# RetNet attention into a mixture of experts on one core: loads of v on ScalarE's queue, and the second routing round in another order

## The chip, the cores and the metric

The kernel runs on one core of a Trainium2 chip. The core has TensorE (PE in the profile, its weight loads PEld), VectorE (DVE), ScalarE (ACT), GpSimd (POOL) and SyncE (SP), and 16 DMA engines that all of its queues share. The metric is the time on the device in microseconds; lower is better. Each engine takes its instructions in the order in which they are written, so an instruction that waits holds back all that stand behind it on its engine; this goes for DMA issues too.

## The reference, cut to what matters

q, k and v are 4 batches x 8 heads x 768 tokens x 64. The attention's output, 3072 tokens of 512 numbers, goes through a gate, which sends each token to one of eight experts.

```python
def _attn_ref(q, k, v):
    gamma = 1.0 - 2.0 ** (-5.0 - np.arange(H))
    for t in range(S):
        state = gamma * state + np.einsum('bhd,bhe->bhde', k[:, :, t], v[:, :, t])
        y[:, :, t] = scale * np.einsum('bhd,bhde->bhe', q[:, :, t], state)

def _moe_ref(x, w_gate, w1, w2):
    logits = x @ w_gate
    expert_idx = np.argmax(logits, axis=1)
    probs = np.exp(logits - logits.max(-1, keepdims=True)); probs /= probs.sum(-1, keepdims=True) + 1e-09
    gate_w = probs[np.arange(N), expert_idx]
    for e in range(E):                                   # x, y sorted by expert
        y[lo:hi] = np.maximum(x[lo:hi] @ w1[e], 0.0) @ w2[e]
    return gate_w[:, None] * y                           # back in the tokens' order
```

## The kernel before, in words

The attention is done in chunks of 128 tokens. A **step** `s` of the loop (12 of them) takes one chunk of two batches, b = 0 and 1. In a step TensorE does, in this order: `scores` (`sc`, both batches), `with_state` (`y` from the state of the chunks before), on odd steps `logits` of two earlier steps (`parts`), `turn_k` for the next step (`trk`), on odd steps the turn of the logits back (`lg`) and `turn_q` for the next two steps (`trq`), `next_state` (`new`), and `within` (`y` from the masked scores and v, in two halves of 16 products). The other engines stand between these:

- **ScalarE** copies from PSUM what TensorE needs next: `qT` and `kT` for `sc`, `lgT` for `lg`, and `xT`, the step's output, from `y`.
- **VectorE** masks the scores (`am`, two for each batch), adds the state, turns `xT` into rows (`to_rows`, `xg`, three buffers) and does the routing.
- **GpSimd** multiplies q and v by powers of the decay (`qs`, `vs`; the last step's v in place), and later gathers rows.
- **SyncE** issues nearly all transfers, one behind the other: two q of 512 KB on odd steps for three steps ahead, two k of 256 KB for three steps ahead, two v of 256 KB for two steps ahead, then `store` of an earlier step's `xg` to `x_d` (four transfers). ScalarE's queue has one transfer before, `dec`, at the start.

A transfer issued from SyncE or ScalarE is given one of eight semaphores (DMAHW0 to DMAHW7), and it is issued only when the transfer that had the semaphore before has landed. Which one that was is decided when the program is built.

Routing goes in three rounds. A round (`place(i)`) is a Python generator that is cut into pieces by `yield`; `WHEN` says at which of a step's places (letters) the next piece is taken. The second round works on the tokens of steps 5 to 8 and runs in steps 9 and 10. Its pieces: the one-hot choice `ohs` and the gate; `rk`, 9 products that count tokens (L703 to L708) and VectorE's ranks behind them; `val` (L737); `here` (L730, 8 instructions); `found`, 8 products (L746); and last `inv` and the row numbers `src_e`, with which GpSimd gathers the early rows and then scales the last step's v.

```python
WHEN = {5: "abc", 6: "b", 7: "ab", 8: "pp", 9: "aw", 10: "nmbb"}
within(s, y, am, early_rows if s + 1 == STEPS else lambda: step(s, "w"))   # "w": between the halves
```

Of the kernel before, what the change touches and what calls it, by code (L numbers as in the profile page):

```python
# [21 lines left out]
P = 128  # L22
# [24 lines left out]
def middle(ap, n):  # L47

    dims = [list(d) for d in ap.ap]
    return bass.AP(tensor=ap.tensor, offset=ap.offset, ap=[dims[0], [0, n]] + dims[1:])  # L50
# [3 lines left out]
def kernel(  # L54
# [11 lines left out]
    nc = tc.nc  # L66
# [13 lines left out]
    STEPS = NT // 2  # L80
    NEXT = (0, 5, 9, STEPS)
    NR = len(NEXT) - 1
# [73 lines left out]
    def more_of_weights1(w1t, e, parts, now):  # L156
        for part in (ts(i, F // parts) for i in now):
            nc.sync.dma_start(w1t[:, :, :, part], w1v[:, ds(e, 1), :, part])
# [323 lines left out]
    with ExitStack() as actx:  # L482
# [19 lines left out]
        def load(nm, s, b, parts=1):  # L502
            m, b1, e = where[s]
            src = {"q": q, "k": k, "v": v}[nm]
            if nm == "q":
                to = att.tile([P, H, 2 * D], F32, tag=nm, name=nm, bufs=4)
                for part in (ts(i, H // parts) for i in range(parts)):
                    nc.sync.dma_start(to[:, part, :], src[2 * b1 + b, part, ts(m, 2 * P), :].rearrange(
                        "h (t e) d -> t h (e d)", e=2))
            else:  # L510
                to = att.tile([P, H, D], F32, tag=nm, name=nm, bufs=8)
                nc.sync.dma_start(to, src[2 * b1 + b, :, ts(2 * m + e, P), :].rearrange("h t d -> t h d"))
            raw[nm, s, b] = to

        def scale_q(s, b, by=nc.gpsimd, parts=1):
# [22 lines left out]
        def pairs_of(tag, bufs, name):  # L538
            return ps(tag, bufs, name).rearrange("p (a t) -> p a t", a=HP)
# [18 lines left out]
        def q_of(s, b):  # L558
            return qT2[b][:, :, ts(where[s][2], P // 2), :].rearrange("p a t e -> p a (t e)")

        def scores(s, b):
            kT, qT = front.pop((s, b)), q_of(s, b)
            sc = [pairs_of("sc", 4, "sc") for _ in range(2)]
            am = [att.tile([P, HP, P], F32, tag=f"am{j}", name=f"am{j}") for j in range(2)]
            for a in range(HP):
                for j in range(2):
                    r = ts(j, D)
                    nc.tensor.matmul(sc[j][:, a, :], lhsT=kT[r, a, :], rhs=qT[r, a, :], start=True, stop=True)  # L568

            def mask():  # L570
                for j in range(2):
                    nc.vector.tensor_tensor(out=am[j], in0=sc[j], in1=middle(causal[:, :], HP), op=ALU.mult)  # L572

            return am, mask
# [55 lines left out]
        def to_rows(s):  # L630
            xg = x["g", s] = keep.tile([P, 2, Q, DT * L], F32, tag="xg", name="xg", bufs=3)
            for b in range(2):
                nc.vector.transpose(xg[:, b, :, :].rearrange("p r (a l) -> p a r l", l=L),
                                    x[s][:, :, b, :].rearrange("p a (r l) -> p a r l", l=L))
# [157 lines left out]
        am = [scores(0, 0)]  # L792
# [15 lines left out]
                copy(out=xTa[:, :, ts(t, P)], in_=tr)  # L808

        rest = iter(())  # L810
        WHEN = {5: "abc", 6: "b", 7: "ab", 8: "pp", 9: "aw", 10: "nmbb"}

        def step(s, at):
            for _ in range(WHEN.get(s, "").count(at)):
                next(rest, None)

        for s in range(STEPS):
            if s + 3 < STEPS:
                if s % 2:
                    load_all("q", s + 3)  # L820
                load_all("k", s + 3)
                load_all("v", s + 2)
            if s % 2 == 0 and s + 2 < STEPS:
                for b in range(2):
                    scale_q(s + 2, b)
            if s + 2 < STEPS and s != NEXT[NR - 1]:
                scale_both(s + 1)
            if s == NEXT[NR - 1] + 1:
                scale_both(s)
            if s in (1, 2):  # L830
                nc.gpsimd.memset(xs2[s % 2], 0.0)
            if s:
                am = [scores(s, b) for b in range(2)]
                step(s, "n")
                for _, mask in am:
                    mask()
                step(s, "m")
            if s + 1 == STEPS:
                pad_ranks(acc[:, NR - 1, 0:2])
            y = outputs()  # L840
            steps = [i for i in (s - 2, s - 1) if i >= 0] if s % 2 else []
            if s + 1 == STEPS:
                logit = logits(steps)
            if where[s][0] or where[s][2]:
                with_state(s, y)

            def ahead():
                for b in range(2):
                    turn_k(s + 1, b)

            def ahead_q():
                if s % 2:
                    for b in range(2):
                        turn_q(s + 1, b)

            if s:
                if s + 1 < STEPS:
                    if steps:
                        logit = logits(steps)
                    ahead()  # L860
                if s + 1 == STEPS:
                    for t in range(HALF):
                        nc.scalar.copy(out=xe[:, t, :].rearrange("p (a q l) -> p q a l", q=Q, l=L),
                                       in_=xs2[0][:, t, :].rearrange("p (q a l) -> p q a l", q=Q, l=L))
                reduce = logits_of(*logit) if steps else lambda: None
                step(s, "p")
                if s + 1 < STEPS:
                    ahead_q()
                to_rows(s - 1)
                reduce()  # L870
                if 2 <= s <= NEXT[NR - 1]:
                    store(s - 2)
                if s == NEXT[NR - 1]:
                    store(s - 1)
                if s + 1 == STEPS:
                    store(s - 1)
                if s + 1 == STEPS:
                    store(NEXT[NR - 1])
                    wa.append(weights2(first, 0, 2, [0]))
                if s == NEXT[NR - 1]:  # L880
                    load_all("v", STEPS - 1)
                    wa = [weights1(first, 0, 4, [0])]
                if s in NEXT:
                    rest = chain(rest, place(NEXT.index(s) - 1))
                step(s, "a")
            next_state(s)
            step(s, "b")
            if s == NEXT[NR - 1] + 1:
                more_of_weights1(wa[0], 0, 4, [1])
                more_of_weights1(wa[0], 0, 2, [1])  # L890
            within(s, y, am, early_rows if s + 1 == STEPS else lambda: step(s, "w"))
            if s == 0:
                ahead()
            step(s, "c")
# [320 lines left out]
```

## Time and profile before

| | us |
|---|---|
| median of 3 runs (lowest, highest) | 444.47 (444.21, 445.1) |
| the profiled execution's own time | 444.41 |
| its span in the trace | 442.3 |
| TensorE busy in the span | 423.5 |
| mean granted clock of TensorE, share of full speed | 0.996 |

The profiled execution's time and the median lie 0.06 us apart; 2.1 us of the time lie outside the span. TensorE is idle for 442.3 - 423.5 = 18.8 us of the span. In the rows below a line reads: start, duration, engine, line, operation, output<-inputs, and in brackets the engine's idle time just before and the work whose end ended it. "SPq" and "ACTq" are transfers' issues on those engines.

### The profile page before, as it was taken

To read this page: it belongs to the slowest core of one execution; us is meant where nothing else is said; L and a number is where in the kernel's file an instruction comes from. 1 tells how busy PE (TensorE), PEld (TensorE's weight loads), DVE (VectorE), ACT (ScalarE), POOL (GpSimd) and SP (SyncE) were. 2 spreads that over 40 slices of the span, in tenths; PEclk is the share of its full clock that TensorE was granted. 3 is DMA by queue.
4 is the path that set the end of the run, shared out by engine and by line. 5 is a ranking of instruction groups with operands and counts; after the bars stand their busy time and mean duration, and the time that the engine had idled before them with its cause. 6 is when DMAs were issued, how large, how long until landed. Compare 5 with 4: busy or idle time off the path is not lost.

```text
span 442.3 us, 9832 instructions
## 1 busy us (share of the span) xinstructions
PE 423.5 (96%) x3643; PEld 371.3 (84%) x3643; DVE 241.8 (55%) x541; ACT 124.4 (28%) x285; POOL 272.5 (62%) x226
## 2 busy tenths in 40 slices
PE   6899999999999999999999999999899999999992
PEld 3798888877688779689989999997899999699681
DVE  3454686979689937624553563365256346433320
ACT  2355355453421211312310221133122123102310
POOL 4458444544137379397548956899795798679011
PEclk9999999999999999999999999999999999999998
DMA  9999998998982799368134951596594268120001
GB/s 195 221 243 210 240 256 184 251 227 206 275 244 77 246 396 350 82 237 283 35 74 116 371 160 45 156 367 146 158 368 113 52 193 307 33 92 0 5 30 53
DMA packets 113324, 80.68 MB, mean 182 GB/s; under 512 B 56874, under 2 KB 97834, under 8 KB 113200
## 3 DMA queue, kind: packets, MB, share of 16 engines
q1 hardware_dynamic: 104336, 65.31, 52.9%
q0 software_dynamic: 5520, 12.60, 8.8%
q10 hardware_dynamic: 3344, 1.36, 1.3%
q8 instruction: 49, 0.80, 0.8%
q14 instruction: 75, 0.61, 0.4%
HBM read 60.88 MB, written 15.99 MB: 174 GB/s over the span
## 4 chain that ended last, share of the span: by engine, by line
PE 80%; DMA 7%; DVE 3%; SPq 3%; issue 2%; ACT 1%; POOL 1%; ACTq 1%; POOLq 0%; DVEq 0%
PE p L343 25%; PE p L389 17%; PE p L277 8%; PE p L264 6%; PE p L979 6%; PE sc L568 4%; PE y L622 3%; SPq L640 2%; PE yp L389 2%; PE new L604 2%; PE trk L536 2%; PE trq L536 2%; DMA x_d<-xg 2%; DMA w2t<-in_moe_w_dram 2%; DMA q<-in_q_dram 1%
## 5 line engine op out<-in xcount | busy, mean ns | idle before, releaser
L177 POOL DMA_INDIRECT xs<-x_d,src x30 | 31.8, 1060 | 19.0 <-issue 7.2
L347 DVE TENSOR_TENSOR hT<-p,q 128x196 f32<-128x196 f32 (+5 forms) x72 | 25.9, 360 | 31.4 <-PE p L343 31.3
L572 DVE TENSOR_TENSOR am<-sc,causal 128x512 f32<-128x512 f32 x48 | 29.9, 682 | 18.1 <-PE sc L568 18.0
L436 POOL DMA_INDIRECT out_dram<-o,dst x20 | 19.9, 996 | 31.1 <-ACT o L285 12.0
L526 POOL TENSOR_TENSOR vs<-v,dec 128x512 f32<-128x512 f32 x21 | 22.8, 1102 | 24.4 <-DMA v<-in_v_dram 21.5
L389 PE MATMUL p<-ws,hs 128*128 128x256 f32 x168 | 37.5, 380 | 0.4 <-issue 0.4
L277 PE MATMUL p<-w2t,hT 128*24 128x128 f32 (+5 forms) x288 | 37.6, 357 | 0.0
L389 PEld LDWEIGHTS p<-ws,hs 128*128 128x128 f32 x168 | 31.9, 190 | 4.9 <-issue 0.7
L343 PE MATMUL p<-t,w1t 128*128 128x196 f32 (+5 forms) x192 | 35.8, 330 | 0.0
L343 PE MATMUL p<-t,s 128*128 128x196 f32 (+5 forms) x192 | 35.8, 330 | 0.0
L395 DVE SCALAR_TENSOR_TENSOR q<-p,gate,q 128x256 f32<-128x256 f32 x28 | 12.9, 480 | 38.2 <-ACT q L404 24.4
L520 POOL TENSOR_TENSOR qs<-q,dec 128x512 f32<-128x512 f32 x22 | 22.3, 1044 | 18.0 <-DMA q<-in_q_dram 10.9
L305 POOL TENSOR_TENSOR ws<-w2t,ws 128x1024 f32<-128x1024 f32 x14 | 33.0, 2360 | 0.5
L305 POOL TENSOR_TENSOR ws<-w2t 128x1024 f32<-128x1024 f32 x14 | 33.1, 2364 | 0.1
L343 PEld LDWEIGHTS p<-t,w1t 128*128 128x128 f32 x192 | 32.4, 190 | 0.0
L343 PEld LDWEIGHTS p<-t,s 128*128 128x128 f32 x192 | 32.4, 190 | 0.0
L277 PEld LDWEIGHTS p<-w2t,hT 128*24 128x24 f32 (+5 forms) x288 | 18.5, 123 | 16.1 <-issue 14.8
L347 DVE TENSOR_TENSOR q<-p,q 128x196 f32<-128x196 f32 (+5 forms) x48 | 17.1, 358 | 25.6 <-PE p L343 18.4
L395 DVE SCALAR_TENSOR_TENSOR o<-p,gate,q 128x256 f32<-128x256 f32 x21 | 10.2, 484 | 35.4 <-PE p L389 35.4
L568 PE MATMUL sc<-qT,kT 64*128 64x128 f32 x384 | 24.9, 279 | 2.3 <-ACT kT L555 2.3
L389 PE MATMUL p<-w2t,hT 128*128 128x256 f32 x112 | 26.9, 382 | 0.1
L568 PEld LDWEIGHTS sc<-qT,kT 64*128 64x128 f32 x384 | 22.5, 188 | 4.6 <-ACT kT L555 3.0
(221 smaller groups left out, 888.3 us busy)
## 6 DMA issues: line engine op xcount, KB each, us to landing
w1t<-in_moe_w_dram SPq DMA_DIRECT2D x7, 2048.0 KB, 8.7
w2t<-in_moe_w_dram SPq DMA_DIRECT2D x7, 2048.0 KB
k<-in_k_dram SPq DMA_DIRECT2D x24, 256.0 KB, 6.0
v<-in_v_dram SPq DMA_DIRECT2D x24, 256.0 KB, 4.3
x_d<-xg SPq DMA_DIRECT2D x48, 128.0 KB, 3.3
q<-in_q_dram SPq DMA_DIRECT2D x11, 512.0 KB, 6.5
xs<-xs SPq DMA_DIRECT2D x80, 64.0 KB, 2.2
w2t<-in_moe_w_dram SPq DMA_DIRECT2D x2, 1024.0 KB
```

The lines of the kernel that those rows point to most:

```text
L177: nc.gpsimd.indirect_dma_start(out=xs[:, t, :], out_offset=None, in_=x_d[0:rows, :], in_offset=bass.IndirectOffsetOnAxis(ap=idx[:, t : t + ...
L264: nc.tensor.matmul(hp, lhsT=w1t[:, 0, dt, ts(f, P)], rhs=xT[:, dt, n0:n], start=(dt == 0), stop=(dt == DT - 1))
L277: nc.tensor.matmul(y[j * z : j * z + m, 0:c], lhsT=hT[:, f, t * P + r0 : t * P + r0 + m], rhs=w2t[:, 0, f, ts(j, c)], start=(i == 0), stop ...
L305: by.tensor_tensor(out=ws[i], in0=sums[i][0], in1=sums[i][1], op=ALU.subtract)
L343: nc.tensor.matmul(rows(y), lhsT=a(d, f), rhs=b(d), start=start and d == 0, stop=d == 1, skip_group_check=True)
L347: nc.vector.tensor_tensor(out=to, in0=rows(y), in1=rows(plus), op=ALU.add)
L389: nc.tensor.matmul(y, lhsT=a[:, f, :], rhs=b[:, f, :], start=start and f == 0, stop=f == FH - 1, skip_group_check=True)
L395: nc.vector.scalar_tensor_tensor(out=to, in0=y, scalar=g[i], in1=plus, op0=ALU.mult, op1=ALU.add)
L526: by.tensor_tensor(out=vs, in0=got, op=ALU.mult, in1=inner(dec[:, ts(NC + 2 * where[s][0] + where[s][2], H)], D))
L568: nc.tensor.matmul(sc[j][:, a, :], lhsT=kT[r, a, :], rhs=qT[r, a, :], start=True, stop=True)
L572: nc.vector.tensor_tensor(out=am[j], in0=sc[j], in1=middle(causal[:, :], HP), op=ALU.mult)
L979: nc.tensor.matmul(y, lhsT=w2t[:, 0, f, ts(dt, P)], rhs=hT[:, f, EARLY : EARLY + m], start=(i == 0), stop=(i == FT - 1))
```

## The change

Three edits. (a) `load` issues v of every step but the last from ScalarE (`nc.scalar`); the last step's v stays on SyncE. (b) `WHEN` and the place of `step(s, "m")` change: in step 9 `rk` goes from between the halves of `within` to behind it; in step 10 `val` goes from ahead of all masks to between the two batches' masks, and `found` and what hangs on it go from ahead of `within` to between its halves. (c) In step 10 `to_rows(9)` and two loads of weights go behind `within`.

```diff
--- before.py
+++ after.py
@@ -509,7 +509,8 @@
                         "h (t e) d -> t h (e d)", e=2))
             else:
                 to = att.tile([P, H, D], F32, tag=nm, name=nm, bufs=8)
-                nc.sync.dma_start(to, src[2 * b1 + b, :, ts(2 * m + e, P), :].rearrange("h t d -> t h d"))
+                queue = nc.scalar if nm == "v" and s + 1 < STEPS else nc.sync
+                queue.dma_start(to, src[2 * b1 + b, :, ts(2 * m + e, P), :].rearrange("h t d -> t h d"))
             raw[nm, s, b] = to
 
         def scale_q(s, b, by=nc.gpsimd, parts=1):
@@ -808,7 +809,7 @@
                 copy(out=xTa[:, :, ts(t, P)], in_=tr)
 
         rest = iter(())
-        WHEN = {5: "abc", 6: "b", 7: "ab", 8: "pp", 9: "aw", 10: "nmbb"}
+        WHEN = {5: "abc", 6: "b", 7: "ab", 8: "pp", 9: "ac", 10: "mnww"}
 
         def step(s, at):
             for _ in range(WHEN.get(s, "").count(at)):
@@ -831,10 +832,10 @@
                 nc.gpsimd.memset(xs2[s % 2], 0.0)
             if s:
                 am = [scores(s, b) for b in range(2)]
+                am[0][1]()
+                step(s, "m")
+                am[1][1]()
                 step(s, "n")
-                for _, mask in am:
-                    mask()
-                step(s, "m")
             if s + 1 == STEPS:
                 pad_ranks(acc[:, NR - 1, 0:2])
             y = outputs()
@@ -866,7 +867,8 @@
                 step(s, "p")
                 if s + 1 < STEPS:
                     ahead_q()
-                to_rows(s - 1)
+                if s != NEXT[NR - 1] + 1:
+                    to_rows(s - 1)
                 reduce()
                 if 2 <= s <= NEXT[NR - 1]:
                     store(s - 2)
@@ -885,10 +887,11 @@
                 step(s, "a")
             next_state(s)
             step(s, "b")
+            within(s, y, am, early_rows if s + 1 == STEPS else lambda: step(s, "w"))
             if s == NEXT[NR - 1] + 1:
+                to_rows(s - 1)
                 more_of_weights1(wa[0], 0, 4, [1])
                 more_of_weights1(wa[0], 0, 2, [1])
-            within(s, y, am, early_rows if s + 1 == STEPS else lambda: step(s, "w"))
             if s == 0:
                 ahead()
             step(s, "c")
```

ScalarE at the start of the program, before (`dec` is the table of decays; in brackets what a row waits for: an engine's work or a transfer's semaphore):

```order
L107 DMA dec<-in_decay_dram 128x96
L549 ACT_TABLE_LOAD
L549 COPY qT<-trq 128x512 [waits PE_49]
L555 COPY kT<-trk 128x512 [waits PE_49]
L549 COPY qT<-trq 128x512 [waits PE_49] x2
L555 COPY kT<-trk 128x512 [waits PE_49]
L625 COPY xT<-y 128x2x2x128 [waits PE_49]
```

and in the changed kernel; the four rows of v are v(0,b=0), v(0,1), v(1,0), and, in a row of its own, v(1,1):

```order
L107 DMA dec<-in_decay_dram 128x96
L513 DMA v<-in_v_dram 128x8x64 x3
L513 DMA v<-in_v_dram 128x8x64 [waits DMAHW1_49]
L550 ACT_TABLE_LOAD
L550 COPY qT<-trq 128x512 [waits PE_49]
L556 COPY kT<-trk 128x512 [waits PE_49]
L550 COPY qT<-trq 128x512 [waits PE_49] x2
L556 COPY kT<-trk 128x512 [waits PE_49]
L513 DMA v<-in_v_dram 128x8x64 [waits DMAHW0_49]
```

Four issues stand ahead of the table load and the first copies of `qT`; the fourth waits for DMAHW1, which the first half of q(0,0) has. The fifth, v(2,0), waits for k(0,1).

ScalarE in steps 2 and 3, from the end of step 1's `xT` on, before:

```order
L628 COPY xT<-y 64x2x2x128 [waits PE_49]
L628 COPY xT<-y 64x2x2x128
L555 COPY kT<-trk 128x512 [waits PE_49,Activation_49] x2
L625 COPY xT<-y 128x2x2x128 [waits DVE_49,PE_49]
L628 COPY xT<-y 64x2x2x128 [waits PE_49]
L628 COPY xT<-y 64x2x2x128
L654 COPY lgT<-parts 128x512 [waits PE_49]
L555 COPY kT<-trk 128x512 [waits PE_49,Activation_49] x2
```

and after; the row with DMAHW6 is v(4,0), for which that semaphore means the landing of q(4,1), and DMAHW0 in the next, v(4,1), means that of k(4,0); the two rows behind step 2's `xT` are v(5,0) and v(5,1), which wait for the first two stores of step 0:

```order
L629 COPY xT<-y 64x2x2x128 [waits PE_49]
L629 COPY xT<-y 64x2x2x128
L513 DMA v<-in_v_dram 128x8x64 [waits DMAHW6_49,DMAHW5_49,Pool_49]
L513 DMA v<-in_v_dram 128x8x64 [waits DMAHW0_49,DVE_49]
L556 COPY kT<-trk 128x512 [waits PE_49,Activation_49] x2
L626 COPY xT<-y 128x2x2x128 [waits DVE_49,PE_49]
L629 COPY xT<-y 64x2x2x128 [waits PE_49]
L629 COPY xT<-y 64x2x2x128
L513 DMA v<-in_v_dram 128x8x64 [waits DMAHW5_49,Pool_49]
L513 DMA v<-in_v_dram 128x8x64 [waits DMAHW7_49,Pool_49]
L655 COPY lgT<-parts 128x512 [waits PE_49]
L556 COPY kT<-trk 128x512 [waits PE_49,Activation_49] x2
```

Two issues now stand ahead of the copies (`xT`, `kT` or `lgT`) of each of steps 0 to 8. Which transfers the later ones wait for: v(6) for v(5,1) and the first store of step 1, v(7) for v(6), v(8) for v(7,1) and the first store of step 3, v(9) for v(8), v(10) for k(10,1) and the second store of step 5.

TensorE from the end of step 9's `within` to step 10's, before:

```order
L622 MATMUL y<-am_1541,vs 64x128
L568 MATMUL sc<-qT,kT 128x128 x16
L591 MATMUL y<-qT,state_1359 64x128 x16
L536 MATMUL trk<-ident,k 128x128 x8
L604 MATMUL new<-vs,k 64x64 x16
L746 LDWEIGHTS here
L746 MATMUL found<-val,here 128x160
```

and after:

```order
L707 MATMUL rk<-ohs,ones_b 128x8
L709 LDWEIGHTS ones_b
L709 MATMUL rk<-acc,ones_b 128x64
L569 MATMUL sc<-qT,kT 128x128 x16
L592 MATMUL y<-qT,state_1359 64x128 x16
L537 MATMUL trk<-ident,k 128x128 x8
L605 MATMUL new<-vs,k 64x64 x16
L623 MATMUL y<-am_1721,vs 64x128
```

`rk` has gone from between the halves (not in the rows of before, 8 products earlier) to just ahead of step 10's `sc`, and `found` no longer follows `new`: the first half of `within` does.

VectorE in step 10, before (`am_1721` to `am_1734` are the masks, the first two of b = 0):

```order
L737 TENSOR_TENSOR val<-at,told 128x1280
L572 TENSOR_TENSOR am_1721<-sc,causal 128x512
L572 TENSOR_TENSOR am_1722<-sc,causal 128x512
L572 TENSOR_TENSOR am_1733<-sc,causal 128x512
L572 TENSOR_TENSOR am_1734<-sc,causal 128x512
L730 TENSOR_SCALAR here<-rrow,prow 128x128 x8
L633 STREAM_TRANSPOSE xg<-xT 128x4x4x32 x2
L610 TENSOR_TENSOR state_1809<-new,state_1359 128x512
L750 TENSOR_TENSOR inv<-inv,found 128x160
L188 TENSOR_SCALAR far_e<-inv 128x2
```

and after:

```order
L573 TENSOR_TENSOR am_1722<-sc,causal 128x512
L738 TENSOR_TENSOR val<-at,told 128x1280
L573 TENSOR_TENSOR am_1733<-sc,causal 128x512
L573 TENSOR_TENSOR am_1734<-sc,causal 128x512
L731 TENSOR_SCALAR here<-rrow,prow 128x128 x8
L611 TENSOR_TENSOR state_1806<-new,state_1359 128x512
L751 TENSOR_TENSOR inv<-inv,found 128x160
L188 TENSOR_SCALAR far_e<-inv 128x2
L189 TENSOR_TENSOR far_e<-inv,far_e 128x2
L190 SCALAR_TENSOR_TENSOR tok_e<-inv,far_e 128x2
L191 TENSOR_SCALAR src_e<-tok_e 128x2
L634 STREAM_TRANSPOSE xg<-xT 128x4x4x32 x2
```

`val` stands between the two batches' masks, and `xg` of step 9 behind the row numbers `src_e`.

## Rows read from the trace of the kernel before

**Rows 1.** From the profile's page: the span, and the engines' busy time.

```profile
span 442.3 us, 9832 instructions
PE 423.5 (96%) x3643; PEld 371.3 (84%) x3643; DVE 241.8 (55%) x541; ACT 124.4 (28%) x285; POOL 272.5 (62%) x226
```

**Rows 2.** Busy time of the engines in three stretches of the span (its length, then PE, PEld, DVE, ACT and POOL, each with its count), then the granted clock, the DMA engines' busy share and GB/s.

```profile
0.00:11.00 11.00, 7.21 (x38) 4.33 (x38) 4.41 (x12) 2.77 (x4) 4.75 (x21) 1.00 0.90 195
11.00:22.00 11.00, 9.39 (x164) 8.30 (x168) 4.59 (x8) 4.25 (x8) 5.09 (x5) 1.00 1.01 221
24.00:57.00 33.00, 33.00 (x588) 29.49 (x586) 16.97 (x28) 17.06 (x32) 20.85 (x19) 1.00 1.02 230
```

**Rows 3.** The first long piece of the chain that ended last: start, us, what.

```profile
2.40 6.37 DMA q<-in_q_dram
```

**Rows 4.** Timeline of the first 10 us: issues on SyncE and ScalarE, and the first work of ScalarE, VectorE and GpSimd.

```profile
0.82 0.45 ACTq L107 DMA_DIRECT2D dec<-in_decay_dram  x1
1.31 1.28 ACT L549 ACT_TABLE_LOAD   x1 [1.31 <-PEq L1201]
...
2.40 0.74 SPq L508 DMA_DIRECT2D q<-in_q_dram  x1
...
3.18 2.39 SPq L512 DMA_DIRECT2D k<-in_k_dram  x1
...
4.21 1.59 DVE L520 TENSOR_TENSOR qs<-q,dec 128x256 f32<-128x256 f32 x4 [2.73 <-DMA q<-in_q_dram]
...
6.08 0.61 ACT L549 COPY qT<-trq 128x512 f32<-128x512 f32 x1 [3.49 <-PE trq L536]
...
8.92 2.04 POOL L520 TENSOR_TENSOR qs<-q,dec 128x512 f32<-128x512 f32 x2 [5.55 <-DMA q<-in_q_dram]
```

**Rows 5.** Packets of the DMA queues from 2.6 to 3.2 us: queue, packets, MB, share of 16 engines. q1 carries SyncE's transfers, q10 ScalarE's.

```profile
q1 hardware_dynamic: 253, 0.13, 73.4%
q10 hardware_dynamic: 128, 0.05, 28.7%
```

**Rows 6.** The same from 3.3 to 3.9 us, the row of q1.

```profile
q1 hardware_dynamic: 417, 0.21, 114.7%
```

**Rows 7.** From the page's list of transfers: count, KB of each, median us from issue to landing.

```profile
k<-in_k_dram SPq DMA_DIRECT2D x24, 256.0 KB, 6.0
...
x_d<-xg SPq DMA_DIRECT2D x48, 128.0 KB, 3.3
q<-in_q_dram SPq DMA_DIRECT2D x11, 512.0 KB, 6.5
```

**Rows 8.** Timeline of steps 2 and 3: SyncE's issues, ScalarE's copies, and the turn of step 0's rows and the scores between them.

```profile
26.13 2.41 SPq L508 DMA_DIRECT2D q<-in_q_dram  x1
...
28.32 1.17 ACT L628 COPY xT<-y 64x512 f32<-64x512 f32 x2 [0.29 <-PE y L622]
28.63 2.93 SPq L512 DMA_DIRECT2D k<-in_k_dram  x2
...
30.93 1.08 ACT L555 COPY kT<-trk 128x512 f32<-128x512 f32 x2 [1.45 <-PE trk L536]
...
31.62 3.08 SPq L512 DMA_DIRECT2D v<-in_v_dram  x2
31.79 1.30 DVE L633 STREAM_TRANSPOSE xg<-xT 128x512 f32<-128x512 f32 x2
...
34.04 2.06 PE L568 MATMUL sc<-qT,kT 64*128 64x128 f32 x32
...
36.80 2.82 SPq L512 DMA_DIRECT2D v<-in_v_dram  x2
...
38.20 0.59 ACT L654 COPY lgT<-parts 128x512 f32<-128x512 f32 x1 [2.87 <-PE parts L651]
```

**Rows 9.** The group of all issues of v: duration in ns, least, median and most, and first and last start.

```profile
L512 SPq DMA_DIRECT2D v<-in_v_dram x24: 422/1040/2664, 5.6 to 103.4; - x24
```

**Rows 10.** Timeline of steps 9 and 10 around the moved work: `rk`, the scores of step 10, GpSimd's products of v, `val`, the masks, `here`, `found`, SyncE's issue of weights, and the scores of step 11.

```profile
96.19 0.19 PE L704 MATMUL rk<-ohs,before 128*128 128x64 bf16 x1 [0.66 <-DVE ohs L686]
...
97.54 2.06 PE L568 MATMUL sc<-qT,kT 64*128 64x128 f32 x32
...
98.28 3.29 POOL L526 TENSOR_TENSOR vs<-v,dec 128x512 f32<-128x512 f32 x2
98.37 2.29 DVE L737 TENSOR_TENSOR val<-at,told 128x1280 bf16<-128x1280 f32 x1
...
100.59 2.47 DVE L572 TENSOR_TENSOR am<-sc,causal 128x512 f32<-128x512 f32 x4
...
102.98 1.38 DVE L730 TENSOR_SCALAR here<-rrow,prow 128x128 bf16<-128x128 bf16 x8
...
103.28 1.38 PE L746 MATMUL found<-val,here 128*128 128x160 bf16 x8 [0.54 <-DVE here L730]
104.26 6.79 SPq L158 DMA_DIRECT2D w1t<-in_moe_w_dram  x3
...
106.48 2.06 PE L568 MATMUL sc<-qT,kT 64*128 64x128 f32 x32
```

**Rows 11.** VectorE in step 8: the first round's `val`, with 1600 numbers a partition.

```profile
77.38 1.80 DVE L737 TENSOR_TENSOR val<-at,told 128x1600 bf16<-128x1600 f32 x1
```

**Rows 12.** TensorE in step 5, ahead of the last turns of q.

```profile
58.17 0.63 PE L536 MATMUL trq<-ident,qs 128*128 128x128 f32 x4 [0.34 <-DVE lg L662]
```

## The prediction, made before the changed kernel ran

> **What bounds the kernel now.** I read the page first: TensorE is busy 423.5 of 442.3 us, and every other engine far less [rows 1]. So the time is TensorE's work plus 18.8 us in which it idles, and the change adds or takes no work of TensorE: the same products run, in another order. It can only move idle time. Where idle time lies in the part that changes I read from the stretches: 3.8 us of it in the first 11 us, 1.6 in the next 11, and none from 24 to 57 us [rows 2]. In that last stretch TensorE has no slack to give, so whatever arrives late there is added to the end, and what is lost at the start is not caught up. The DMA engines are busy for about the whole of all three stretches (shares 0.90, 1.01, 1.02 [rows 2]): in the attention a transfer that is moved ahead pushes another back.
>
> Next the chain that ended last: it begins with the transfer of q(0,1), from 2.40 to 8.77 us [rows 3]. GpSimd waits 5.55 us for it and starts `qs` at 8.92 [rows 4]; everything of batch 1 hangs on that. Then I looked at how the two queues behave together. From 2.6 to 3.2 us ScalarE's one transfer, `dec`, ran beside SyncE's, and SyncE's queue moved 253 packets while `dec` moved 128 [rows 5]; in an equal time without it SyncE's queue moved 417 [rows 6]. The sum is nearly the same (381 and 417): two queues share one supply. Last, the moved work's own places: the timelines of steps 2 and 3 [rows 8] and of steps 9 and 10 [rows 10].
>
> **A, the start: +3.0.** ScalarE's `dec` issue ends at 1.27 [rows 4], and an issue of v takes 0.42 us at least [rows 9]. So v(0,0) is on its way by 1.7, v(0,1) by 2.1 and, if there is room, v(1,0) by 2.5, while q(0,1) is only issued at 2.40 to 3.14 [rows 4]. Before, all v came behind it. SyncE's data up to q(0,1)'s end occupy the time from about 2.7 to 8.77, 6.1 us. With a third of the packets going to the other queue (128 of 381) SyncE gets 253/381 = 0.66, and 6.1 becomes 9.2: +3.1. The limit from the other side is what three tiles need: 0.79 MB at 195 to 221 GB/s [rows 2] is 3.6 to 4.0 us. I take 3.0, near the row that shows two queues together; bounds 0 (v gets only gaps) and 4.0 (all three tiles go first).
>
> The Trainium skill, "DMA: Bandwidth & Descriptors", section "Queues, rings and completion order", says that a DMA engine goes round the queues that have work, a packet from each. Equal turns would give the upper end, 4.0, and a sum 1.0 higher; the 128 packets in rows 5 were all that `dec` had, so no row here tells a third from a half.
>
> A second lateness lies beside the first and is not added. ScalarE's fourth issue, v(1,1), waits for the first half of q(0,0), which has landed when VectorE starts at 4.21 [rows 4]. An issue can also be slow when much is under way: SyncE's fifth took 2.39 us [rows 4]. So ScalarE is free between 4.6 and 6.6, then loads its table (1.28, until now hidden in idle time), and copies the first `qT` at 5.9 to 7.9 in place of 6.08. At most 1.8 us late, inside the 3.0 for which TensorE waits for q(0,1) anyway. If that cover is gone, it costs up to 1.8 by itself.
>
> **B, ScalarE behind SyncE's landings: +1.8.** Each of steps 0 to 8 now has two issues ahead of its copies, each waiting for an earlier transfer, mostly SyncE's. All the copies that TensorE waits for stand behind them. Steps 2 and 3, in the times of before, with TensorE 3.0 later by A and transfers not (the engines that carry them were full already):
>
> Step 2: ScalarE ends `xT` at 29.49 [rows 8]. v(4,0) waits for q(4,1): issued at 26.13, 6.5 us to landing [rows 7], 32.6. v(4,1) waits for k(4,0): 28.63 + 6.0 = 34.6. With one more issue at the median of 1.04 [rows 9] ScalarE is free at 35.7 and ends the two `kT` (1.08) at 36.7. TensorE wants them at 34.04 + 3.0 = 37.0. Just in time; with the first product waiting for `kT` and for buffers I put 0.3.
>
> Step 3: v(5) waits for the first two stores of step 0. With two pairs of v gone from SyncE (3.08 + 2.82 us of issue [rows 8]) these are no longer issued near 39.7 but when `xg` is ready, 33.1 + 3.0 = 36.1, and land 3.3 us behind their issue [rows 7]; the second of them at about 40.5. Two issues bring ScalarE to 41.5 to 42.6, where `lgT` was due at 38.20 + 3.0 = 41.2: late by 0.3 to 1.4, and `lg` follows it directly. I put 0.9.
>
> Steps 4 to 8: v(7) and v(9) wait for v alone, one step old; their two issues, 2.1 us, fit into the idle time of 2.87 ahead of `lgT`. v(6) and v(8) wait for a store of an older step. I put 0.6 for all. Bounds: 0 (all in the idle time) and 3.9 (0.9 in three odd steps, 0.3 in four even).
>
> **C, the second round's order: -0.8.** `rk` waits 0.66 us for `ohs` [rows 10]. With the second half of `y` ahead of it, TensorE has work until 96.6, `ohs` is there, and the scores of step 10 start at 96.9, not 97.54. But VectorE's ranks start after `rk`, 0.4 later than before. So the first masks start at 98.37 + 0.4 = 98.8, take 1.24 (half of 2.47) to 100.0; `val` takes 2.29 as now, or 1.44 where GpSimd's products don't run beside it (round 1 took 1.80 for 1600 numbers [rows 11], here 1280), to 101.5 or 102.3; the other masks to 102.7 or 103.5; `here` to 104.1 or 104.9; `found` ends 0.2 behind, and the second half of `y`, 1.1, brings TensorE to step 11's scores at 105.4 to 106.2, against 106.48. That is -0.3 to -1.1; I take -0.8, as most of GpSimd's pair is over by then. Bounds 0, and -2.1: both waits (0.66, 0.54) and `val`'s slow part (0.85) gained.
>
> Edit (c) at nothing: `xg` of step 9 (1.3 us) now follows the row numbers, which the gather wants first. Its store stands behind the weights' issue, which ends at 104.26 + 6.79 = 111.05 [rows 10], so a turn ending near 107.6 is in time; the loads keep their place on SyncE. Without that cover step 11's masks, behind `xg`, lose the gain, which is C's bound of 0.
>
> **D, SyncE relieved: -0.3.** 22 issues of about 1.04 us leave SyncE. Step 5's wait of 0.34 for late rows [rows 12] should go, as stores are issued earlier. Bounds 0 and -0.3.
>
> **Sum.** 444.41 + 3.0 + 1.8 - 0.8 - 0.3 = 448.1 us. It starts from the profiled execution, 0.06 below the median.
>
> **The rivals.** *ScalarE's waits are hidden*: A without B, 446.3. For it: idle times of 1.45 and 2.87 ahead of `kT` and `lgT` [rows 8]; against: those are shorter than the landings worked out above. *The waits pile up*: A at 3.6, B at its bound, 450.8; for it, that a late ScalarE delays `xT`, so stores, on which v waits again.
>
> *The other side, faster*: the v queue takes only turns that SyncE leaves. Then q(0,1) lands at 8.8 as before, no wait of B ends later than ScalarE's idle time, and C and D are left: 443.3. It decides at A + B below 1.1. The sum of packets in rows 5 and 6 speaks against it, the idle time of ScalarE for it. The Trainium skill, same page, section "Issuing engines are not separate DMA queues", says that issuing from several engines saves only the sequencer's time; that would leave the transfers' time unchanged and give this rival, or the next. *Nothing moves*: SyncE's saved issues pay for ScalarE's, 444.4.
>
> **Chances and range.** Forecast, 446.8 to 450: 0.50. Hidden waits: 0.20. Pile-up: 0.10. Faster: 0.12. Nothing: 0.08. A measurement of this kernel tells 0.2%, 0.9 us, from no change. So slower 0.80, same 0.08, faster 0.12. The range reaches from the unchanged time, 444.2, to 451.5 (A at 4.0 and B near its bound), which leaves out the faster rival and a few hundredths above.
>
> **What would show it.** A: GpSimd's first `qs` starts near 12, not 8.92, with three v landed before it; wrong if below 9.5. B: in steps 2 and 3 ScalarE's idle time ahead of `kT` and `lgT` ends by a transfer, and TensorE waits for `kT` or `lgT` for 0.3 to 1.4 us between 30 and 50; wrong if TensorE is as full there as before. C: no wait ahead of `rk`; step 11's scores start about 0.8 less behind step 9's than now. D: no wait of `trq` for `lg` in step 5. The forecast fails most easily at A, whose size hangs on how the engines divide themselves between queues in the first 10 us.

## The result

The changed kernel takes 447.07 us (median of 8 runs, lowest 446.29) where the kernel before takes 444.34 on the same chip: ratio 1.0057, 95% interval 1.0031 to 1.0082. A second measurement (below, after_again) gave 448.59 against 444.32, 1.0093 (1.0068 to 1.0117). So it is slower, by 2.7 and 4.3 us in the medians; 448.1 was forecast. Some executions run several us longer at a lower granted clock: the ratios leave them out, and of the traces below only order_only's is of such a one. The way to the forecast time was not quite the forecast one.

The page of the changed kernel, its span and busy times (to [rows 1]):

```profile
span 445.4 us, 9831 instructions
PE 425.1 (95%) x3643; PEld 372.3 (84%) x3643; DVE 244.7 (55%) x541; ACT 123.9 (28%) x285; POOL 271.2 (61%) x226
```

The same three stretches as in [rows 2], after:

```profile
0.00:11.00 11.00, 6.86 (x34) 3.89 (x34) 3.27 (x11) 2.37 (x3) 2.90 (x20) 1.00 0.98 200
11.00:22.00 11.00, 8.57 (x108) 7.36 (x110) 4.28 (x6) 4.67 (x8) 5.34 (x5) 0.84 1.30 238
24.00:57.00 33.00, 31.26 (x544) 27.13 (x534) 16.62 (x28) 15.77 (x29) 22.93 (x22) 1.00 1.11 243
```

TensorE was full from 24 to 57 us and now idles for 1.74 of them; in the stretch from 11 to 22 its granted clock is 0.84, a share of the time at half (1.2 GHz), where it was 1.00. Its busy time grew by 1.6 us, for the most part for that reason: the turns of q and k behind 11.90 us took 3.2 us there, against 1.9 before.

Where the time goes is seen best in how late each step starts. The table gives the start of TensorE's scores in each step, and of the early rows' first products (L264, `hp`), in us later than in the kernel before's first trace (12.86 for step 0's batch 1; 18.79, 28.20, 34.04, 44.09, 50.97, 61.98, 87.06, 97.54 for steps 1 to 6, 9, 10; 115.70 for `hp`). All are read from timelines of TensorE; "before, again" (before_again below) shows what a repetition alone moves; "changed, again" is after_again.

| kernel | 0, b1 | 1 | 2 | 3 | 4 | 5 | 6 | 9 | 10 | hp |
|---|---|---|---|---|---|---|---|---|---|---|
| changed | 2.69 | 2.69 | 3.85 | 4.32 | 5.38 | 5.37 | 4.83 | 5.59 | 4.58 | 5.22 |
| changed, again | 1.79 | 1.79 | 3.96 | 4.43 | 6.07 | 7.88 | 7.34 | 7.45 | 6.43 | 6.41 |
| before, again | -0.61 | -0.61 | -0.61 | -0.61 | -0.60 | -0.61 | -0.03 | -0.02 | -0.59 | -0.59 |
| v_only | 1.92 | 1.92 | 4.24 | 4.44 | 6.29 | 8.10 | 7.57 | 7.67 | 6.81 | 7.06 |
| v_start | 2.58 | 4.06 | 4.06 | 4.05 | 4.06 | 4.06 | 3.52 | 3.39 | 2.66 | 2.61 |
| v_later | -0.54 | -0.54 | 5.56 | 5.56 | 7.08 | 7.08 | 6.54 | 6.62 | 5.60 | 5.47 |
| v_shift | 1.83 | 1.83 | 3.74 | 3.74 | 5.53 | 5.93 | 5.39 | 5.43 | 4.41 | 4.63 |
| v_near | -0.06 | -0.06 | 1.66 | 1.66 | 3.29 | 7.51 | 6.97 | 7.05 | 6.04 | 6.37 |
| v_six | -0.71 | -0.70 | -0.24 | -0.24 | -0.24 | -0.04 | 5.22 | 5.09 | 4.23 | 4.03 |
| after_warm | 1.83 | 1.84 | 3.73 | 4.02 | 5.35 | 5.34 | 4.81 | 4.92 | 3.91 | 4.21 |
| order_only | -0.18 | -0.18 | -0.18 | -0.18 | -0.17 | -0.18 | 3.71 | 3.72 | 2.84 | 3.11 |
| order_again | -0.43 | -0.43 | -0.39 | -0.39 | -0.39 | -0.39 | -0.38 | -0.37 | -1.25 | -1.73 |
| order_third | -0.56 | -0.56 | -0.56 | -0.56 | -0.55 | -0.56 | -1.00 | -1.00 | -1.87 | -1.72 |

The changed kernel loses 2.69 us by step 1 and as much again by step 4. At 121 us it is 5.2 late, and at the end 3.1 (spans 445.4 and 442.3).

**The start.** Timeline of the changed kernel, rows that answer to [rows 4]:

```profile
1.30 5.89 ACTq L513 DMA_DIRECT2D v<-in_v_dram  x4
...
2.39 0.95 SPq L508 DMA_DIRECT2D q<-in_q_dram  x1
...
7.22 1.28 ACT L550 ACT_TABLE_LOAD   x1 [7.22 <-issue]
...
10.81 2.04 POOL L521 TENSOR_TENSOR qs<-q,dec 128x512 f32<-128x512 f32 x2 [7.44 <-DMA q<-in_q_dram]
...
11.90 2.12 PE L537 MATMUL trq<-ident,qs 128*128 128x128 f32 x8 [1.09 <-POOL qs L521]
```

The four issues of v hold ScalarE until 7.19, the table load follows, and `qs` of batch 1 starts at 10.81, 1.89 later than before. Then the eight turns of q take 2.12 us, where the two groups of four took 0.66 each: the clock has fallen. Granted clock is the column before the DMA share:

```profile
12.00:13.00 1.00, 1.00 (x5) 0.71 (x6) 1.00 (x2) 0.00 (x0) 1.00 (x2) 0.50 1.39 218
13.00:14.00 1.00, 1.00 (x6) 1.00 (x6) 0.40 (x1) 0.64 (x1) 1.00 (x1) 0.50 1.38 218
```

Ahead of the fall TensorE had waited 1.40 us for k(0,0), 0.94 for `kT` and 1.09 for `qs`. So 2.69 is 1.89 of transfer and 0.80 that come behind it, with half clock. Packets, MB and share of the two queues from 4 to 7 us (as [rows 5]), and in the last row SyncE's queue in the same 3 us before:

```profile
q1 hardware_dynamic: 1267, 0.37, 67.9%
q10 hardware_dynamic: 1423, 0.36, 65.9%
...
q1 hardware_dynamic: 2134, 0.81, 115.8%
```

Here the queues take turns of about one to one, and together they move 0.74 MB where SyncE's queue alone moved 0.81: more packets, but smaller ones (before, 1071 of 2134 were under 512 bytes, now 2466 of 2690 are). The same from the start to the landing of q(0,1): in the changed kernel to 10.66 us, taken as 0.15 ahead of `qs` as in the trace before, and in the last row SyncE's queue before, to 8.77:

```profile
q1 hardware_dynamic: 3183, 1.32, 54.9%
q10 hardware_dynamic: 3128, 0.80, 41.7%
...
q1 hardware_dynamic: 4608, 1.68, 83.5%
```

q(0,0), k(0,0) and q(0,1) are 1.31 MB. So 0.75 MB of v (0.80 less `dec`), nearly three tiles, now go ahead of q(0,1)'s end, but 0.36 MB of SyncE's own later transfers, which used to run beside it, no longer do. That leaves 0.39 MB more in 1.89 us.

**Steps 1 to 3.** Timeline of the changed kernel, ScalarE and TensorE:

```profile
25.14 1.50 ACTq L513 DMA_DIRECT2D v<-in_v_dram  x2
26.68 0.37 ACT L655 COPY lgT<-parts 128x256 f32<-128x256 f32 x1 [4.76 <-DMA k<-in_k_dram]
...
42.61 1.01 ACTq L513 DMA_DIRECT2D v<-in_v_dram  x2
43.66 0.58 ACT L655 COPY lgT<-parts 128x512 f32<-128x512 f32 x1 [4.01 <-PE trk L537]
```

```profile
26.28 0.66 PE L537 MATMUL trk<-ident,k 128*128 128x128 f32 x4 [0.46 <-DMA k<-in_k_dram]
27.10 0.44 PE L662 MATMUL lg<-ident,lgT 128*128 128x128 f32 x2 [0.16 <-ACT lgT L655]
...
44.30 0.66 PE L662 MATMUL lg<-ident,lgT 128*128 128x128 f32 x4 [0.83 <-ACT lgT L655]
```

In step 3 the copy `lgT` stands behind two issues of v that start at 42.61, and TensorE waits 0.83 us for it: the forecast wait at the forecast place. The bracket of the copy's row names the products `trk`, which run beside it; the chain that ended last (start, us, what) names what held the second issue, a store that landed at 42.99:

```profile
37.07 5.92 DMA x_d<-xg
...
43.08 0.54 ACTq L513
...
43.66 0.59 ACT lgT L655
```

In step 1 there are two waits: for k(2,1) itself, and for a `lgT` that stands behind issues which wait for a landing of k.

**The second round.** Rows of steps 9 and 10 of the changed kernel, to [rows 10]:

```profile
101.78 0.20 PE L705 MATMUL rk<-ohs,before 128*128 128x64 bf16 x1
...
102.23 0.23 DVE L711 TENSOR_TENSOR own<-rk,ohs 128x64 f32<-128x64 f32 x1 [0.53 <-PE rk L709]
...
103.02 2.07 POOL L527 TENSOR_TENSOR vs<-v,dec 128x512 f32<-128x512 f32 x2
103.08 1.02 DVE L722 TENSOR_SCALAR prow<-ranks 128x8 int32<-128x8 int32 x1
...
104.23 1.15 DVE L724 TENSOR_TENSOR at<-ohs,is_col 128x256 f32<-128x256 bf16 x1
...
105.30 1.27 DVE L573 TENSOR_TENSOR am<-sc,causal 128x512 f32<-128x512 f32 x2
...
108.63 0.43 PE L623 MATMUL y<-am,vs 128*64 128x128 f32 x2 [0.88 <-DVE am L573]
```

`rk` and `found` no longer wait, but TensorE waits 0.88 us for the second batch's masks. `ohs` was there at 100.04, so here `rk` could have run between the halves without a wait; behind both halves it comes late, VectorE waits for it, and its small instructions then meet GpSimd's products of v: `prow` takes 1.02 and `at` 1.15 us. In the second trace of the kernel before, with the same products starting after them, they take 0.16 and 0.42:

```profile
96.88 0.16 DVE L721 TENSOR_SCALAR prow<-ranks 128x8 int32<-128x8 int32 x1
...
97.25 0.42 DVE L723 TENSOR_TENSOR at<-ohs,is_col 128x256 f32<-128x256 bf16 x1
```

### The profile page after: what moved, and what is told of

Same layout as the page of the kernel before. It is cut to its first block, busy times and chain, and to the rows that moved or that the text cites. A ratio compares the mean times of both kernels' runs of the same rounds, so it can differ in the third digit from the quotient of the medians.

```text
span 445.4 us, 9831 instructions
## 1 busy us (share of the span) xinstructions
PE 425.1 (95%) x3643; PEld 372.3 (84%) x3643; DVE 244.7 (55%) x541; ACT 123.9 (28%) x285; POOL 271.2 (61%) x226
## 4 chain that ended last, share of the span: by engine, by line
PE 78%; DMA 8%; SPq 4%; issue 3%; DVE 2%; POOL 2%; ACT 1%; ACTq 0%; POOLq 0%; DVEq 0%
PE p L343 25%; PE p L389 19%; PE p L277 8%; PE p L264 6%; PE p L982 6%; PE hp L264 3%; PE yp L389 3%; PE y L623 2%; DMA v<-in_v_dram 2%; DMA k<-in_k_dram 2%; DMA q<-in_q_dram 2%; PE sc L569 1%; DMA x_d<-xg 1%; PE new L605 1%; PE trq L537 1%
```

## Experiments

All names stand in the table above. Times are compared within a group of runs, which had one chip: the first four runs, the next four, v_near to order_again, and order_third (the first group's chip, an hour later). The kernel before took 448.0, 444.3, 448.2 and 443.1 us in them, and in the first and third its times spread widely (443.9 to 453.4, 444.7 to 449.4), so the traces up to 121 us carry the argument.

**order_only**: the changed kernel, with

```diff
-                queue = nc.scalar if nm == "v" and s + 1 < STEPS else nc.sync
+                queue = nc.sync
```

> The new order of the second round with every v on SyncE's queue. Theory (the change's three terms are independent): the attention up to step 9 is as in the kernel before, step 11's scores start 0.3 to 1.1 us earlier relative to step 9's, and the time is 443.3 to 444.1 against 444.34. Rival (the order gives nothing, since VectorE's ranks, val and masks take the place of the two waits): no wait ahead of rk, but a wait for the masks of about 1 us ahead of the first half of y in step 10, and the time is within 0.3 us of the kernel before.

Measured: ratio 1.0015 (0.9976 to 1.0055). Nothing is lost up to step 5. There the last turns of q waited 2.6 us for `lg`, which on VectorE stood behind rows that waited for a store (the same wait is 0.34 and 0.93 in the two traces of the kernel before); the order has no part in that. From step 9 to `hp` it takes 28.03 us, against 28.64 and 28.07 in the two traces of the kernel before; TensorE waits 0.9 us for the masks of step 10, as the rival said.

**v_only**: the kernel before, with edit (a) alone.

> Only the queue of v is changed (all but the last step's on ScalarE's queue), the second round in its old order. Theory: all of the loss is here. Step 1's scores start 2.7 us later than in the kernel before, step 4's 5.4 later, expert products at 200 us about 5 to 6 later; time 447 to 448. Rival (the loss comes from the new order, or needs both): time within 1 us of the kernel before.

Measured: ratio 1.0137 (1.0089 to 1.0186), 453.76 us against 448.0. All of the loss is in the queue's change. It was larger than the 447 to 448 expected; in part that is a stop of 1.5 us in the middle of step 4's scores (see after_again).

**v_start**: the kernel before, with

```diff
+                queue = nc.scalar if nm == "v" and s < 2 else nc.sync
```

> Old order; only the four v of steps 0 and 1 are on ScalarE's queue, all later ones on SyncE's. Theory (the start and ScalarE's later waits are separate costs): step 1's scores start 2.5 to 2.9 us later than in the kernel before, TensorE's clock falls to half for some 3 us near 12 to 15 us as in the changed kernel, and from there to step 4 nothing more is lost (less than 0.5). Rival (what is lost in steps 1 to 3 also follows from the start, because the queues' order of landing is upset there): step 4's scores are over 4 us late here too.

Measured: ratio 1.0041 (0.9999 to 1.0083). 2.58 late at step 0's second scores, 4.06 at step 1's, nothing more behind: the theory, with a dearer half clock. It held from 12 to past 18 us, granted clock in two of these:

```profile
15.00:16.00 1.00, 0.56 (x4) 0.56 (x6) 0.00 (x0) 0.39 (x1) 0.00 (x0) 0.50 1.30 188
16.00:17.00 1.00, 1.00 (x14) 1.00 (x12) 0.00 (x0) 0.00 (x0) 0.00 (x0) 0.50 1.17 272
```

The 16 products of the scores took 2.08 us in place of 1.16.

**v_later**: the changed kernel, with the condition `2 <= s < STEPS - 1`, so that v of steps 0 and 1 is on SyncE's queue.

> The changed kernel with the four v of steps 0 and 1 back on SyncE's queue; v of steps 2 to 10 stays on ScalarE's. Theory: step 1's scores start as in the kernel before (within 0.3), clock full there; from step 1 to step 4 TensorE loses 2 to 4 us, since ScalarE's copies stand behind issues that wait for SyncE's landings and TensorE is not 2.7 us late to hide a part of them. Rival (those losses follow from the start): less than 0.7 lost up to step 4.

Measured: 450.11 and 451.96 us against 448.0, too few for an interval. The start is as before and 6.1 us are lost in step 1 alone, 1.5 in step 3. More than the theory's 2 to 4, and the rival falls too. TensorE's rows in step 1:

```profile
23.26 0.66 PE L537 MATMUL trk<-ident,k 128*128 128x128 f32 x4 [1.35 <-DMA k<-in_k_dram]
24.29 0.66 PE L537 MATMUL trk<-ident,k 128*128 128x128 f32 x4 [0.37 <-DMA k<-in_k_dram]
...
27.15 0.52 PE L662 MATMUL lg<-ident,lgT 128*128 128x128 f32 x2 [2.21 <-ACT lgT L655]
27.47 3.53 PE L537 MATMUL trq<-ident,qs 128*128 128x128 f32 x16
```

k late, 1.7 us; `lgT` late, 2.2; and the turns of q at half clock, 3.53 in place of 1.91. In the changed kernel, which is 2.7 us late by then, step 1 loses 1.2.

**before_again**: no edit.

> The kernel before, unchanged, profiled again beside the changed one on one chip. Theory (the waits of 1.24 and 0.36 us that its trace shows at 316 and 228 us are its own): they come again, and the early rows' second products start near 131.4 us. Rival (they are chance): one or both are gone or others have come.

Measured: ratio 0.9984 (0.9949 to 1.0019). The wait for `ofr` at 316 us came again:

```profile
315.80 1.65 PE L343 MATMUL p<-xT,w1t 128*128 128x208 f32 x8 [0.84 <-DMA ofr<-xTa]
```

It was 1.24 in the first trace; the wait at 228 us was gone. The wait of `rk` for `ohs` was gone too.

**after_again**: no edit to the changed kernel.

> The changed kernel, unchanged, profiled again. Theory: the early rows' second products start 4.5 to 6 us later than in the kernel before of the same chip, with the clock at half between about 12 and 15 us, and the time is 2 to 5 us above it. Rival (the 5.2 us at 131 us were chance): less than 3 us there.

Measured: ratio 1.0093 (1.0068 to 1.0117). 6.4 late at `hp`, 7.0 against the same chip's trace of the kernel before. The clock stayed full here from 11 to 22 us, against the theory, and step 0's second scores were 1.79 late, not 2.69. What it lost instead is a stop within one run of 16 products, for which the profile names nothing:

```profile
53.31 0.72 PE L569 MATMUL sc<-qT,kT 64*128 64x128 f32 x8 [1.55 <-issue]
```

**after_warm**: the changed kernel, with `warm(256)` ahead of `turn_k(0, 0)` and of `turn_q(0, 1)`; the products' results are not used.

> The changed kernel with two more products of idle numbers (128x256) on TensorE in the first 12 us, one ahead of the turn of k(0,0), one ahead of the turn of q(0,1), where it waits anyway. Theory (the clock fell because TensorE idled from 6.7 to 11.9 us with little between): the clock stays full from 12 to 15 us, and step 1's scores start 0.6 to 1.0 us earlier than in the changed kernel. Rival (the clock falls anyway, or the products come in the way): step 1's scores start no earlier, or later.

Measured: ratio 1.0063 (1.0039 to 1.0087). The clock stayed full and the second scores came 0.86 earlier than in the changed kernel's first trace. But after_again had a full clock without the two products and was as early, so this doesn't show that they kept it up.

**v_shift**: the changed kernel, with `load_all("v", s + 2)` moved to just ahead of `next_state(s)`.

> The changed kernel with the issues of v in steps 1 to 8 moved, in ScalarE's order, from the top of a step to behind its copies of lgT, kT and qT (the transfers, their queue and the landings they wait for stay in kind). Theory (ScalarE's copies stand behind issues that wait): TensorE's waits for lgT and kT in steps 1 to 4 go, and step 4's scores start 1.5 to 2.7 us earlier than in the changed kernel; what is left of the loss is the start's 2.7. Rival (what is lost there is the transfers themselves: k lands later because v shares the engines): step 4's scores start within 0.7 us of the changed kernel's.

Measured: ratio 1.0059 (1.0039 to 1.0079). Step 4's scores are 5.53 late, within 0.7 of the changed kernel: by the numbers the rival. But its waits show both causes:

```profile
25.68 0.66 PE L537 MATMUL trk<-ident,k 128*128 128x128 f32 x4 [1.40 <-DMA k<-in_k_dram]
26.56 0.66 PE L537 MATMUL trk<-ident,k 128*128 128x128 f32 x4 [0.22 <-DMA k<-in_k_dram]
...
40.37 0.44 PE L592 MATMUL y<-qT,state 64*64 64x128 f32 x4 [0.54 <-ACT xT L626]
41.56 1.09 PE L592 MATMUL y<-qT,state 64*64 64x128 f32 x28 [0.76 <-ACT xT L629]
```

In step 1, k itself is late. In step 3 the waiting issues now hold back `xT` in place of `lgT`: they run from 38.35 to 39.63 us, the copy follows at 39.73, and TensorE waits for that. (The profile names step 3's masks as the end of ScalarE's wait; they end at 39.67, but this copy is step 2's, and in the changed kernel it runs 1.8 us ahead of them.) A place that is free of charge was not found by moving the issues within a step.

**v_near**: v_later, with v of the next step asked for in place of that of the next but one:

```diff
-                load_all("v", s + 2)
+            if 1 <= s < STEPS - 2:
+                load_all("v", s + 1)
```

> As the kernel in which only v of steps 2 to 10 is on ScalarE's queue (new order), but each of these v is asked for one step later (one step ahead of its use, not two); the issues still stand ahead of a step's lgT and kT. That kernel lost 7.1 us up to step 4's scores. Theory (what is lost in steps 1 to 3 is k's landing: v on a second queue passes k, which is needed first): k(2) and k(3) land in time, TensorE doesn't wait for k in step 1, and at most 1.5 us are lost up to step 4's scores. Rival (ScalarE's copies held back by issues that wait for SyncE's landings): TensorE still waits for lgT and kT, and 2 us or more are lost.

Measured: ratio 1.0036 (0.9998 to 1.0075). In step 1 TensorE waits neither for k nor for `lgT`; it waits 1.4 us for GpSimd's products of v(1), 1.7 lost against 6.1. Up to step 4's scores 3.3 are lost, by the number the rival. In step 3 the other cause stands alone, TensorE and ScalarE:

```profile
42.21 0.66 PE L662 MATMUL lg<-ident,lgT 128*128 128x128 f32 x4 [1.40 <-ACT lgT L655]
```

```profile
40.48 1.05 ACTq L513 DMA_DIRECT2D v<-in_v_dram  x2
41.57 0.59 ACT L655 COPY lgT<-parts 128x512 f32<-128x512 f32 x1 [4.58 <-DMA x_d<-xg]
```

ScalarE stood until a store had landed. So the theory holds for step 1 and the rival for step 3. The 4.2 us from step 4 to 5 are a stop of 2.4 us in the midst of step 4's scores, again with no cause named, and half clock behind it.

**v_six**: the kernel before, with the condition `6 <= s < STEPS - 1`.

> Old order of the second round; only v of steps 6 to 10 on ScalarE's queue, all others on SyncE's. Theory (what the change loses is lost before step 4, and from there SyncE's relief gains): up to step 5's scores as in the kernel before; the wait of the last turns of q in step 5 for late rows (0.3 to 0.9 us) goes, nothing is lost behind it; the early rows' first products start 0.3 to 1.0 us earlier than in the kernel before, the time is 0.3 to 1 us lower. Rival (issues on ScalarE cost at every step): some 0.3 us lost at each of steps 4 to 8, 1 us or more later in all.

Measured: ratio 1.0057 (1.002 to 1.0093); the theory falls. Unchanged up to step 5, and there 5.3 us lost at one place:

```profile
59.32 0.59 ACT L655 COPY lgT<-parts 128x512 f32<-128x512 f32 x1 [6.27 <-DMA x_d<-xg]
```

```profile
59.96 0.72 PE L662 MATMUL lg<-ident,lgT 128*128 128x128 f32 x4 [3.74 <-ACT lgT L655]
60.47 3.56 PE L537 MATMUL trq<-ident,qs 128*128 128x128 f32 x16
```

v(7)'s two issues run from 55.61 to 59.28 us, and the profile names the landing of a store as the end of ScalarE's wait. SyncE's queue, which still carries k and v of the early steps, is late with it, and `lgT` waits behind: 3.7 us, and 1.6 more since the turns then ran at half clock. The two issues of step 4 cost 0.2. So the wait on another queue's landing is a cost by itself, as large as that queue happens to be late.

**order_again** and **order_third**: order_only, twice more.

> The new order of the second round alone, all v on SyncE's queue, once more, since on the first chip its trace had a long wait for rows in step 5 that has nothing to do with the order. Theory (the order gives its 0.3 to 1.1 us): from step 9's scores to the early rows' first products 0.3 us or more less than in the kernel before's second trace (28.07 us). Rival (it gives nothing: where the wait for ohs is absent, the masks of step 10 take back what the wait for here gave): within 0.3 us of 28.07.

> The new order alone for a third time, all v on SyncE's queue: is this part by itself a kernel that beats both? From step 9's scores to the early rows' first products the two runs so far show 28.03 and 27.28 us; old orders show 27.58 to 28.64. Theory (a small gain): again 27.3 to 28.0, and the time 0.3 to 1.2 us below the kernel before. Rival (nothing): 28.0 or more, the time within 0.3 us of it or above.

Measured: ratios 0.9969 (0.9935 to 1.0003) and 1.0002 (0.9987 to 1.0017); 27.28 and 27.92 us from step 9 to `hp`. The five traces with the old order took 27.58 to 28.64 (mean 28.04), the nine with the new one 27.28 to 28.27 (mean 27.81): they overlap. Only order_again, where `ohs` came 0.2 us ahead of `rk` and the masks cost no wait above 0.2, shows what was hoped for. order_third's 27.92 lies in the theory's 27.3 to 28.0, its time is the rival's. TensorE's longest wait in this stretch of order_third is the one that took its place:

```profile
PE y L623 <- DVE am L573: 1.1, 2, 0.9
```

None of the versions tried is shown to beat the kernel before.

## Why the forecast held, step by step

The time fell in the range and in the likeliest case, but the sum was right because errors cancelled: in the first trace A and B come to 6.3 us where 4.8 were forecast, C gave 0.4 of its 0.8, and 2.1 us that stand in no term came back behind 200 us. That the number came out is in part luck.

- **A, +3.0**: the place and kind were right. The two traces show 2.69 and 1.79 (2.40 against the second trace of before), so the term was somewhat large. The third of the packets was wrong: turns were about one to one (1423 to 1267). Yet the transfer cost 1.89, not the 4.0 of equal turns: nearly three tiles did go ahead, as that bound has it, but SyncE's own transfers behind q(0,1) gave way for about half of that (0.36 of 0.75 MB). The reckoning had counted their time as that of q(0,1) and what stands ahead of it. The half clock, 0.8 of the 2.69, stood in no term. The late table load stayed covered, as said: the first `qT` is copied at 8.51 in place of 6.08, and TensorE waits for `qs` to 11.90 all the same. The Trainium skill ("DMA: Bandwidth & Descriptors", "Queues, rings and completion order") says that a DMA engine goes round the queues that have work, a packet from each; the packets of the trace agree, the price drawn from it did not come.
- **B, +1.8**: 2.7 in the first trace (step 1 to 4) and 0.9 in step 8, 4.3 in the second (step 1 to 4). The named mechanism is real (v_near, v_six, step 3's wait). For step 3, 0.3 to 1.4 were worked out and 0.83 and 1.16 measured, though not by its parts: the store took 5.92 us to land, not 3.3, and TensorE was 4.3 late there, not 3.0, which largely cancels. What failed is step 1, which I did not work out: v on a second queue passes k, which is needed first (v_later 1.7 us, v_shift 1.6, v_near none). The reckoning took it for granted that transfers are not late; k's were.
- **C, -0.8**: nothing clear of chance. The 0.66 was the wait of one trace: `ohs` was late for rows that waited for a store, and in the second trace `rk` does not wait. The 0.54 came again there; the new order removes it, but the masks' 0.88 takes its place. The step that failed is VectorE's chain behind `rk`: the first masks start 3.2 us behind the scores (105.30 and 102.12), where 1.9 were worked out (98.8 and 96.9), since `prow` and `at` now meet GpSimd's products and take 1.6 us longer (`val`, now clear of them, takes 1.47 in place of 2.29). The bound of 0, stated for another reason, is where it came out. The Trainium skill ("SBUF — State Buffer", "Who interferes with whom") says that VectorE, in the modes that use two ports, and GpSimd contend for a shared pair: whoever issues first has it for the whole instruction, the other is blocked. The 1.02 us of `prow`, as long as one product of GpSimd (1.04), agree; its mode no run shows.
- **D, -0.3**: the wait went, 0.54 between steps 5 and 6 in the changed kernel and in all but v_six that have v on ScalarE. That SyncE's relief is the cause is not shown: v_start, where only the first four v leave its queue, has the same 0.54. There TensorE is 4.1 us late, which may give the rows time by itself.
- **Not in the sum**: 5.2 late at 200 us, 3.1 at the end. The lateness falls at two places, near 228 us (by 0.6) and at 316 us (by 1.4). At 316 the first trace of before waits 1.24 us for `ofr` (0.84 in the second, 0.84 in order_only, 0.65 in order_third, none in order_again); none of the nine traces with v on ScalarE has that wait. I count this as given back; why they don't have it is open. At 228 before waits 0.36 without a named cause, order_only and order_third too, its own second trace not, and I can't tell that from chance.

In the first trace A is 2.7, B 2.7 to step 4 and 0.9 more in step 8 (`found` waits 1.0 us for `kT`, before 0.3), D -0.5, steps 6 and 7 -0.1, step 9 to `hp` -0.4, and -2.1 is given back: 3.2, and the spans differ by 3.1. Not settled: whether the stops within step 4's scores (1.5 to 2.4 us, three traces, the same product each time) belong to the change. They were seen only with v on ScalarE. Packets of the instruction queues moved about then, but they did so in the kernel before too, without a stop.

## To carry to other kernels

A second queue added little bandwidth here (13.28 MB in the first 57 us against 12.67), but it changed who goes first: v, needed later, passed q and k. So put on it what may land late without harm to the rest. An issue on a busy engine costs more than its 0.4 us when it must wait for another queue's landing; ask which landing that is, and what is queued behind. And count a wait seen in one trace of the kernel before as a gain only if it comes again in a second, and even then look for the wait that stands behind it.

## Not expected of the hardware

A wait of TensorE can cost twice: after waits of 2.2 and 3.7 us the 16 turns behind took 3.5 us in place of 1.9 at a granted clock near 0.5, and after waits of 0.7 to 1.6 us it fell in one trace of the changed kernel and not in the other. Two full queues moved a quarter more packets in 3 us than SyncE's alone (2690 and 2134), but fewer bytes (0.74 and 0.81 MB), since more of them were under 512 bytes.
